# RWKV-style attention and a maxout-like layer on one core: the exponential for k' moved into the PSUM bank of the sums, fp32 sums for three units, a new order

## The chip, the cores and the metric

One core of a Trainium2 chip runs the whole computation as one program. The metric is the device time of the program in microseconds (us), the median of several runs, inputs and outputs in the chip's HBM. TensorE is PE in the profile (its weight loads PEld), VectorE is DVE, ScalarE is ACT, GpSimd is POOL and SyncE is SP; SP issues every DMA of this kernel from one queue, in order.

## The reference

There are 4 batches, 8 heads, 768 tokens and 48 channels a head. A state of 48 x 48 a head runs over the tokens; its output feeds a layer of width 1024.

```python
for t in range(S):                      # S = 768
    cur = einsum('bhd,bhe->bhde', u[None] * kt, vt)
    y[:, :, t] = einsum('bhd,bhde->bhe', rt, state + cur)
    state = wt[..., None] * state + einsum('bhd,bhe->bhde', kt, vt)
x  = y as [B*S, H*D]                    # 3072 x 384
h1 = x @ w1 ; h2 = x @ w2               # 384 x 1024 each
out = maximum(h1, h2) @ w_out           # 1024 x 384
```

All of it is fp32 in HBM; w lies between 0.80 and 0.95.

## The kernel before

The tokens go in three segments of 256, and the work in eight *units* (`UNITS`): units 0 to 3 are segment 0 of one batch each, units 4 and 5 are segment 1 of two batches each, 6 and 7 are segment 2. Two neighbouring tokens share a partition, so that a unit with one batch is one 128-partition tile. Unit 0 alone is worked in two halves of its heads.

For a unit, the steps have short names that the order below uses; the first number behind the name is the unit.

- `load` brings w, k, r, v (384 KB each and batch). `wp` multiplies the two w of a partition, `ln` takes the logarithm in place (tile lg). For units 3 to 7 (`TWO_PARTS`) `hi` and `lo` split that logarithm into two fp16 parts (L200, L202, L413), and the prefix sum `ex` is two fp16 matmuls with a triangular matrix that add up in one PSUM bank (L395, L396); for the others it is one fp32 matmul (L398). 
- `mz` adds the logarithm itself to the sum and puts it in the SBUF tile MZ (L440). `e0` takes the exponential of the sum in place, in the bank (L436); `ie` takes the exponential of minus MZ into the SBUF tile iE (L460). 
- `rw` and `kw` multiply r and k by w for one of the two tokens. `scale` with a 0 makes r' = r times the exponential in the bank (tile rp); `scale` with a 1 makes k' = k times iE (tile kp). 
- `rk`, `ru`, `dg`, `dd`, `di` make the term with u: r k u, summed over channels, put on the diagonal of the mask tile M.
- r' and k' are transposed, on PE with a copy by ACT (`tr`, `te`, tile RK) for units 0 to 4, by DMA on SP's queue (`dt`, L582) for units 5 to 7. `sc` multiplies them (L641), `mk` copies the product under a mask into M on DVE (L650), `ya` multiplies M with v (L688), `yi` adds the state's part (L675), `kv`, `st`, `sm`, `sb` carry the state on. `vb` casts v to bf16.
- `xe` copies the unit's output to xT. The layer follows: max(h1, h2) = h2 + relu(h1 - h2), so `gt` multiplies xT with the difference w1 - w2 (`wdiff`, tile wd_sb; L706), `rl` takes the relu, and `op` adds xT times a folded matrix wc_sb (w2 times w_out; L725) and the relu times w_out (L729) in one bank. `oe` copies it out, `os` stores it.

PSUM has four single banks G (prefix sums, transposes, `gt`, `op`, preparation) and two pairs Y (`sc`, `kv`, the output). In the kernel before, the pools hand the buffers of a tag out.

The list `ORDER` sets the order of the whole program, written out by hand: each word is a step, and each engine takes its own instructions in that order, so what stands ahead on an engine's queue goes first. `@d`, `@a` and `@p` pick DVE, ACT or POOL for a step that may run on more than one; `load`, `dt` and `os` stand on SP's queue.

Of the kernel before, what the change touches and what calls it, by code (L numbers as in the profile page):

```python
# [54 lines left out]
load.0.w.1 load.0.w.0 wp.0.0@d hot.8.2 hot.8.3 load.2.w.0 zero.v.1@d wp.0.1@d mask ln.0.0 tri
zero.k.1@p load.1.w.0 ln.0.1 ex.0.0 load.1.r kw.0.0@d mz.0.0 wp.2.0@d rw.0.0@d load.1.k zero.o@p
load.0.v ie.0.0 uspread utake@a wp.1.0@d ex.0.1 ln.1.0 wload.1.0 mz.0.1 scale.0.1.0.0@p hot.8.0
zero.M.1@p ie.0.1 load.3.w.0 ru.0.0@d dg.0 rw.0.1@p kw.0.1@p scale.0.1.0.1@p wt.0.0 ex.1.0 we.0.0
e0.0.0 e0.0.1 wt.0.1 rk.1.0@d hot.8.5 vb.0.1@p load.2.r zero.v.2@d load.2.k load.1.v mz.1.0 ie.1.0
rw.1.0@d wt.1.0 wload.1.2 ln.2.0 ex.2.0 vb.0.0@a we.0.1 scale.0.0.0.0@d zero.k.0@d kv.0  # L60
scale.0.0.0.1@d tr.0.0.1 dd.0@p mz.2.0 woload.0 we.1.0 ru.1.0@p kw.1.0@p row.2 w2turn.0.0 e0.1.0
scale.1.0.0.0@d st.0.0@a tr.0.0.0 te.0.0.1@a sc.0.0.1.1 sc.0.0.0.1 w2turn.0.1 dg.1 te.0.0.0@a
w2take.0.0@a wload.0.2 load.2.v scale.1.1.0.0@d dd.1@p sb.0.0@a wp.3.0@p tr.1.0.1 e0.2.0 st.0.1
te.1.0.1@a rk.2.0@d zero.M.2@p di.0.0@d ie.2.0 zero.M.0@p rw.2.0@d hot.8.1 wload.1.1 ru.2.0@d
kw.2.0@p scale.2.1.0.0@p sc.0.0.1.0 sc.0.0.0.0 mk.0.0.1.0 vb.1.0@a hot.8.4 mk.0.0.0.0 mk.0.0.1.1
mk.0.0.0.1 vb.1.1@a kv.1 scale.2.0.0.0@d tr.1.0.0 ln.3.0 te.1.0.0@a w2turn.2.1 wdiff.2@p sb.0.1@a
st.1.0@a sb.1.0@a di.1.0@d st.1.1 tr.2.0.0 w2take.0.1@a tr.2.0.1 te.2.0.1@a zero.v.0@d sc.1.0.1.0
w2turn.1.0 wload.0.0 wdiff.0@p w2take.1.0@a sc.1.0.0.0 mk.1.0.1.0 mk.1.0.0.0 sb.1.1@a w2take.2.1@d
w2turn.2.0 w2turn.1.1 w2take.2.0@a hi.3@a ya.0.0.1.0 vb.2.1@a ya.1.0.0.0 sm.0@p sm.1@p wload.0.1
wdiff.1@d ya.1.0.1.0 ya.0.0.0.1 load.3.r trih@a yi.1.0 yi.0.0 ya.0.0.0.0 woload.1 ya.0.0.1.1  # L70
xe.1.0@a xe.0.0@d load.3.k te.2.0.0@a gt.1.3 rl.1.3@a dg.2 rk.3.0@d lo.3@d dd.2@a gt.0.2 rl.0.2@a
wocast.1@p gt.1.1 w2take.1.1@d woload.3 gt.0.0 rw.3.0@p woload.2 rl.0.0@a gt.1.2 load.4.w.0 rl.1.2@a
vb.2.0@p ru.3.0@p gt.0.3 rl.0.3@a ex.3.0 wocast.3@d wocast.2@a wocast.0@a rl.1.1@a di.2.0@d
sc.2.0.1.0 mk.2.0.1.0 gt.0.1 mz.3.0 e0.3.0 kw.3.0@p gt.1.0 dg.3 sc.2.0.0.0 kv.2 st.2.0@a rl.0.1@a
wp.4.0@d ie.3.0 scale.3.0.0.0@d mk.2.0.0.0 wfold.2 sb.2.1@d wfold.0 dd.3@p ln.4.0 load.3.v st.2.1
wfold.1 sb.2.0@d vb.3.0@a wl.2 hi.4@a lo.4@d ya.2.0.0.0 load.4.r rl.1.0@a di.3.0@d vb.3.1@a row.3
ya.2.0.1.0 wctake.1@a we.2 load.4.k wctake.2@a rk.4.0@d wctake.0@a scale.3.1.0.0@p tr.3.0.0 ex.4.0
mz.4.0 tr.3.0.1 ex.4.1 mz.4.1 te.3.0.0@a kv.3 te.3.0.1@a st.3.0@a yi.2.0 xe.2.0@d ie.4.0 op.1.1
oe.1.1@a st.3.1 load.4.v e0.4.0 sb.3.0@a ru.4.0@d gt.2.0 load.5.w.0 rl.2.0@a sc.3.0.0.0 sc.3.0.1.0
vb.4.1@a gt.2.2 op.1.0 rk.4.1@p rw.4.0@d kw.4.0@d scale.4.0.0.0@d scale.4.1.1.0@d scale.4.1.0.0@p  # L80
e0.4.1 rl.2.2@a scale.4.0.1.0@d op.0.1 sb.3.1@a row.4 oe.1.0@a tr.4.1.0 te.4.1.0@a tr.4.1.1 vb.4.0@a
op.0.0 sm.2@p wl.3 mk.3.0.0.0 ya.3.0.0.0 mk.3.0.1.0 ya.3.0.1.0 yi.3.0 oe.0.1@d ru.4.1@p wp.5.0@p
we.3 sm.3@p te.4.1.1@a gt.2.1 xe.3.0@a dg.4 ln.5.0 oe.0.0@d tr.4.0.1 te.4.0.1@a gt.3.0 rl.3.0@a
rl.2.1@a hi.5@a dd.4@d load.5.k kv.4 di.4.0@d sc.4.1.1.0 load.5.r load.5.v rk.5.0@d gt.2.3 rl.2.3@a
gt.3.2 tr.4.0.0 di.4.1@d te.4.0.0@a mk.4.1.1.0 gt.3.3 st.4.0 st.4.1 os.1.0 rl.3.3@a gt.3.1 rl.3.1@a
ru.5.0@p sc.4.1.0.0 rk.5.1@p sc.4.0.0.0 load.6.r sb.4.0@a vb.5.1@a op.2.1 load.6.w.0 lo.5@d wl.4
ex.5.0 mk.4.0.0.0 os.0.0 sb.4.1@a mk.4.1.0.0 oe.2.1@a mz.5.0 e0.5.0 rw.5.0@p ex.5.1 sc.4.0.1.0
load.6.k ru.5.1@p mz.5.1 ya.4.0.0.0 scale.5.0.0.0@d op.2.0 rl.3.2@a op.3.0 mk.4.0.1.0 e0.5.1 os.1.1
scale.5.0.1.0@d dt.5.0.0 ya.4.0.1.0 dt.5.0.1 kw.5.0@d row.5 oe.3.0@d os.3.0 wp.6.0@p ie.5.0
# [708 lines left out]
```

## Time and profile before

| | |
|---|---|
| median of 3 runs | 146.45 us (146.37 to 147.02) |
| the profiled execution | span 147.2 us, 5536 instructions |
| PE busy | 136.8 us (93%) |
| DVE busy | 116.9 us (79%) |
| ACT busy | 90.6 us (62%) |
| POOL busy | 90.0 us (61%) |
| granted TensorE clock, mean | 0.987 |
| DMA | 31.84 MB, mean 216 GB/s |

A busy share is a mean over the span. Matmuls overlap and their ends are modelled: a row's mean duration of one is longer than the step from one to the next. A line number is that of the kernel before; the order and the notes on the change give lines of the changed kernel, which are 9 higher in the functions quoted above.

### The profile page before, as it was taken

What the parts mean: (1) busy time and instruction counts of PE and PEld (TensorE: products, weight loads), DVE (VectorE), ACT (ScalarE), POOL (GpSimd) and SP (SyncE); (2) the same over time, 40 slices, a digit from 0 to 9 for tenths busy, and PEclk for the clock granted to TensorE, in tenths of its full rate; (3) what the DMA queues carried; (4) which work ended last, traced back from release to release, by engine and by line L of the source; (5) the groups of instructions that cost most, each with busy time, mean ns of one, the idle gap of its engine ahead of it and who ended that gap; (6) DMA issues with size and microseconds to landing.
All of it is one profiled execution on the core that took longest, in us unless ns stands there. A gap on an engine that the chain in (4) does not pass through costs nothing.

```text
span 147.2 us, 5536 instructions
## 1 busy us (share of the span) xinstructions
PE 136.8 (93%) x2403; PEld 84.2 (57%) x2404; DVE 116.9 (79%) x162; ACT 90.6 (62%) x164; POOL 90.0 (61%) x106
## 2 busy tenths in 40 slices
PE   5999999779999999999999994999999999999990
PEld 1355755568757666875654562554557545664560
DVE  2489999999999999999999967399967589361511
ACT  4053793997999849999178677367357483227010
POOL 7659979996986299499785909506996900000000
PEclk9999999999999999999999999599999999999999
DMA  4999999999899899997978999799933990051014
GB/s 104 323 325 357 335 401 394 366 286 304 214 241 277 212 226 282 312 255 174 205 192 177 292 251 207 141 138 291 250 136 78 131 271 20 0 210 62 4 56 157
DMA packets 71186, 31.84 MB, mean 216 GB/s; under 512 B 66293, under 2 KB 70390, under 8 KB 71162
## 3 DMA queue, kind: packets, MB, share of 16 engines
q1 hardware_dynamic: 71162, 31.49, 81.2%
q8 instruction: 19, 0.31, 0.8%
q14 instruction: 5, 0.04, 0.2%
...
## 4 chain that ended last, share of the span: by engine, by line
PE 41%; DVE 35%; issue 6%; POOL 6%; DMA 4%; ACT 3%; SPq 2%; DVEq 0%; POOLq 0%; ACTq 0%
PE G L729 12%; DVE M L650 9%; PE G L706 8%; PE G L234 7%; PE G L725 5%; DVE rp L176 4%; DMA lv<-in_v_dram 4%; DVE rku L176 3%; DVE dg L502 3%; POOL kp L180 3%; DVE M L516 3%; PE Y L688 2%; SPq L582 2%; POOL rku L180 2%; PE Y L675 2%
## 5 line engine op out<-in xcount | busy, mean ns | idle before, releaser
L729 PE MATMUL G<-wo_sb,gT 128*128 128x384 bf16 x192 | 35.8, 331 | 0.0
L706 PE MATMUL G<-xT,wd_sb 128*128 128x256 bf16 (+1 forms) x192 | 34.4, 326 | 0.7 <-ACT xT L168 0.6
L650 DVE CAST_PREDICATED M<-mask,Y 128x1024 bf16<-128x1024 int32 (+1 forms) x26 | 28.6, 1131 | 2.8 <-PE Y L641 1.9
L717 ACT ACTIVATE gT<-G 128x512 bf16<-128x512 f32 x43 | 24.5, 601 | 9.8 <-PE G L706 9.6
L729 PEld LDWEIGHTS <-gT 128*128 128x128 bf16 x192 | 19.0, 99 | 12.6 <-issue 0.3
L706 PEld LDWEIGHTS <-wd_sb 128*128 128x128 bf16 x192 | 17.9, 98 | 12.6 <-DVE wd_sb L176 0.6
L180 POOL TENSOR_TENSOR kp<-lk,iE 128x384 bf16<-128x384 f32 x16 | 17.1, 1096 | 9.3 <-DVE lk L176 4.2
L725 PE MATMUL G<-wc_sb,xT 128*128 128x384 bf16 x72 | 15.7, 327 | 0.0
L180 POOL TENSOR_TENSOR rku<-rku,u_b 128x384 f32<-128x384 f32 x14 | 14.5, 1053 | 2.0 <-DVE rku L176 2.0
L234 PE MATMUL G<-S_b 128*128 128x512 bf16 x47 | 13.6, 442 | 1.8 <-DVE S_b L263 1.8
L168 ACT COPY RK<-G 128x1024 bf16<-128x1024 bf16 x12 | 12.1, 1019 | 4.7 <-PE G L565 4.7
L168 ACT COPY osb<-G 128x384 f32<-128x384 f32 x7 | 3.4, 479 | 15.9 <-PE G L729 12.6
L180 POOL TENSOR_TENSOR rku<-lr,lk 128x384 f32<-128x384 f32 x8 | 10.9, 1393 | 2.5 <-DMA lk<-in_k_dram 1.7
L641 PE MATMUL Y<-RK 48*64 48x128 bf16 x384 | 9.0, 220 | 2.6 <-DVE M L650 2.4
L502 DVE TENSOR_REDUCE dg<-rku 128x16 f32<-128x768 f32 x12 | 11.0, 945 | 0.1
L641 PEld LDWEIGHTS <-RK 48*64 48x64 bf16 x384 | 6.2, 106 | 7.8 <-issue 6.7
L168 ACT CAST xT<-Y 128x768 bf16<-128x768 f32 x7 | 7.0, 1025 | 5.3 <-PE Y L675 4.0
L168 ACT CAST S_b<-S_f 64x768 bf16<-64x768 f32 (+1 forms) x14 | 8.7, 624 | 2.3 <-DVE S_f L612 2.0
L176 DVE TENSOR_TENSOR rp<-lr,G 128x768 bf16<-128x768 f32 (+2 forms) x11 | 8.8, 799 | 1.4 <-ACT G L436 1.4
L234 PEld LDWEIGHTS <-S_b 128*128 128x128 bf16 x48 | 5.1, 112 | 8.3 <-issue 3.3
L516 DVE TENSOR_TENSOR M<-identq,gd 128x512 int32<-128x512 int32 x12 | 9.2, 778 | 0.4 <-POOL gd L168 0.3
L168 DVE CAST xT<-Y 128x768 bf16<-128x768 f32 x5 | 5.1, 1017 | 5.5 <-PE Y L688 3.2
...
## 6 DMA issues: line engine op xcount, KB each, us to landing
...
out_dram<-osb SPq DMA_DIRECT2D x14, 192.0 KB, 3.9
...
out_dram<-wb SPq DMA_DIRECT2D x10, 192.0 KB, 2.0
...
```

Source lines behind the costliest of these rows:

```text
L168: (nc.scalar.copy if e == "a" else nc.vector.tensor_copy if e == "d" else nc.gpsimd.tensor_copy)(o, i)
L176: op(o, a, b)
L180: op(o[:, g], a[:, g], b[:, g])
L234: nc.tensor.matmul(t, zz[:, 0:P], zz[:, 0:512], start=True, stop=True)
L502: nc.vector.reduce_sum(s.dg[:, b].rearrange("p i h -> p h i"), s.rku[:, b], axis=AX.X)
L516: (nc.vector if en == "d" else nc.gpsimd).tensor_tensor(out=o, in0=m, in1=g.unsqueeze(3).to_broadcast([P, 2, H, Q // 2]), op=ALU.bitwise_and)
L641: nc.tensor.matmul(t[q * Q:(q + 1) * Q, e, p * P:(p + 1) * P].rearrange("s (i g) -> s i g", i=2), s.kT[d, b, j, y * n + p, q, :], s.rT[d, ...
L650: nc.vector.copy_predicated(t[:, :, 2 * n * y:2 * n * (y + 1)].rearrange("s i (p e) g -> s p e i g", e=2), mask[:, j].bitcast(I32).unsquee ...
L706: nc.tensor.matmul(t[:, m * n * P:(m + 1) * n * P].rearrange("c (b t) -> c b t", t=P), wd_sb[:, ko, fo * P:(fo + 1) * P], s.xT[:, 0:n, ko, :],
L717: nc.scalar.activation(o, i, AF.Relu)
L725: nc.tensor.matmul(t[:, 0:HD], s.xT[:, a, ko, :], wc_sb[:, ko, :], start=(ko == 0), stop=False)
L729: nc.tensor.matmul(t[:, 0:HD], s.gT[:, c:c + P], wo_sb[:, f, :], start=False, stop=(f == FO - 1))
```

## The change

Three tables and the list change, and the code that hands out PSUM. `E_IN_PSUM` now names units 4 to 7: their `ie` writes the exponential of minus MZ for one batch over the sums, into the bank, once r' of that batch has been made (a branch that was in the code, L458 of the changed kernel), and k' of the batch is scaled from the bank. Since POOL reads no PSUM here, all `scale` steps of these units stand on DVE. `TWO_PARTS` names units 6 and 7 alone, so units 3, 4 and 5 take the fp32 matmul and have no `hi` and `lo`. `PLACES` says for each PSUM tile in turn which of the four banks or two pairs it takes. `ORDER` is new as a whole, with the engine of many steps.

```diff
-BANKS = {'G': 4, 'Y': 2}
+PLACES = {
+    'G': ("0123003123120312132120310310303010123012030301203123123021010320310230210130123213201303"
+           "0231203120121301201321320"),
+    'Y': ("01011101011101010110010010101010110100101010"),
+}
...
-E_IN_PSUM = ()
+E_IN_PSUM = (4, 5, 6, 7)
...
-TWO_PARTS = (3, 4, 5, 6, 7)
+TWO_PARTS = (6, 7)
...
 ORDER = """
-ident zero.s.1@p identq@a load.0.k load.0.r zero.m@p identb@p u zero.s.0@d zero.r@d rk.0.0@d
...
+tri zero.o@p mask zero.m@p ident identb@p zero.s.0@d hot.8.5 load.0.w.1 wp.0.1@d zero.M.2@d ln.0.1
...
+    places = {tag: iter(x) for tag, x in PLACES.items()}
+
+    def place(tag):
+        return tag + next(places[tag])
+
     def bank(dt=F32, tag="G"):
-        return ps.tile([P, 512 if dt is F32 else 1024], dt, tag=tag, name=tag, bufs=BANKS[tag])
+        return ps.tile([P, 512 if dt is F32 else 1024], dt, tag=place(tag), name=tag, bufs=1)
 
     def pair(tag="Y"):
-        return ps.tile([P, 2, 512], F32, tag=tag, name=tag, bufs=BANKS[tag])
+        return ps.tile([P, 2, 512], F32, tag=place(tag), name=tag, bufs=1)
```

The order at three places. First DVE at the start of the program, before:

```order
L263 MEMSET S_b 128x768
L249 MEMSET rp_73 128x32x8
L176 TENSOR_TENSOR rku<-lr,lk 128x768
L176 TENSOR_TENSOR lg<-lw 128x192
L254 MEMSET vp_77 128x8x2x8
L255 MEMSET vp_77 128x8x2x8
L176 TENSOR_TENSOR lg<-lw 128x192
L176 TENSOR_TENSOR lw<-lk,lw 128x4x48
L440 TENSOR_TENSOR MZ<-G,lg 128x4x48
```

and of the change:

```order
L272 MEMSET S_b 128x768
L185 TENSOR_TENSOR lg<-lw 128x192
L266 MEMSET M_82 128x512
L449 TENSOR_TENSOR MZ<-G,lg 128x4x48
L185 TENSOR_TENSOR lw<-lr,lw 128x4x48 x2
L185 TENSOR_TENSOR rp_73<-lr,G 128x4x48
L185 TENSOR_TENSOR rp_73<-lw,G 128x4x48
```

The first work on loaded data was r times k of unit 0 and is now the product of the w of half of its heads; that half of w is also the first load on SP, where k and r were, and k is the sixth.

Second SP's queue from the transposes of unit 5 (RK written from rp0 and kp1) to the load of v for unit 6 (lv), with buffer numbers, before:

```order
L582 DMA_TRANSPOSE RK_1678<-rp0_73 128x8x128 x2
L472 DMA row_1714<-MZ_83 1x1024
L743 DMA out_0_dram<-osb_1716 128x384
L743 DMA out_0_dram<-wb_1583 128x384
L582 DMA_TRANSPOSE RK_1678<-kp1_75 128x8x128 x2
L372 DMA lv_2032<-in_v_dram 128x8x96 x2
```

and of the change:

```order
L591 DMA_TRANSPOSE RK_1525<-rp0_73 128x8x128
L381 DMA lk_1604<-in_k_dram 128x8x96 x2
L752 DMA out_0_dram<-osb_1324 128x384
L591 DMA_TRANSPOSE RK_1525<-kp1_75 128x8x128
L381 DMA lr_1771<-in_r_dram 128x8x96 x2
L481 DMA row_1848<-MZ_83 1x1024
L591 DMA_TRANSPOSE RK_1525<-rp0_73 128x8x128
L591 DMA_TRANSPOSE RK_1525<-kp1_75 128x8x128
L752 DMA out_0_dram<-osb_1944 128x384
L381 DMA lv_2078<-in_v_dram 128x8x96 x2
```

The transposes now go batch by batch, and k, r and v of unit 6 (lk, lr, lv) stand among and behind them; before, w, k and r of unit 6 were issued ahead of all of it and v alone behind it.

Third DVE around the scaling of unit 6, before, where r' is the only scaling in these rows:

```order
L176 TENSOR_TENSOR lk_1609<-lk_1609,lw_1570 128x16x48
L516 TENSOR_TENSOR M1_81<-identq_79,gd_1820 128x2x256
L176 TENSOR_TENSOR lr_1553<-lr_1553,lw_1570 128x16x48
L176 TENSOR_TENSOR rp0_73<-lr_1553,G_2025 128x16x48
L650 COPY_PREDICATED M1_81<-mask_71,Y_2068 128x8x2x64
L650 COPY_PREDICATED M1_81<-mask_71,Y_2196 128x8x2x64
L176 TENSOR_TENSOR rp0_73<-lr_1553,G_2038 128x16x48
```

and of the change:

```order
L659 COPY_PREDICATED M1_81<-mask_71,Y_2025 128x8x2x64
L659 COPY_PREDICATED M1_81<-mask_71,Y_2042 128x8x2x64
L185 TENSOR_TENSOR rp0_73<-lr_1771,G_2014 128x16x48
L449 TENSOR_TENSOR MZ_83<-G_2061,lg_1703 128x8x48
L185 TENSOR_TENSOR kp0_74<-lk_1604,G_2014 128x16x48
L177 CAST xT_2205<-Y_2110 128x6x2x64
L185 TENSOR_TENSOR rp0_73<-lr_1771,G_2061 128x16x48
L177 COPY osb_2314<-G_2286 128x384
L728 TENSOR_SCALAR gT_2316<-G_2298 128x512
L185 TENSOR_TENSOR kp0_74<-lk_1604,G_2061 128x16x48
```

k' stands on DVE behind r' of its batch and reads the same bank (G_2014, G_2061); before it stood on POOL and read iE. The products of r and k with w, which stood here on DVE, went to POOL.

More of the change, by code (lines that the diff above doesn't have):

```diff
@@ L53 @@
 ORDER = """
-ident zero.s.1@p identq@a load.0.k load.0.r zero.m@p identb@p u zero.s.0@d zero.r@d rk.0.0@d
[L55 to L89, printed above, removed]
@@ new lines @@
+load.2.k wp.2.0@d hot.8.0 wload.1.1 zero.k.1@p wload.1.2 wload.1.0 ie.1.0 wload.0.2 wload.0.1
+wload.0.0 tr.0.0.1 te.0.0.1@a kw.0.0@d zero.v.2@p scale.0.1.0.0@p wt.1.0 we.1.0 vb.0.1@a vb.0.0@a
+vb.1.0@a load.3.k ru.0.0@d dg.0 hot.8.2 load.3.r vb.1.1@a sc.0.0.1.1 sc.0.0.0.1 identq@d rw.1.0@d
+dd.0@p di.0.0@d woload.0 scale.1.0.0.0@d tr.0.0.0 kv.0 te.0.0.0@a st.0.0@a mk.0.0.1.1 zero.s.1@d
+mk.0.0.0.1 st.0.1 hot.8.1 zero.v.1@p sc.0.0.0.0 rk.1.0@d ru.1.0@d sc.0.0.1.0 woload.1 dg.1 dd.1@d
+kw.1.0@p sb.0.0@a scale.1.1.0.0@p kv.1 tr.1.0.1 ln.2.0 ex.2.0 mz.2.0 row.2 te.1.0.1@a zero.v.0@p
@@ new lines @@
+wdiff.1@d gt.0.1 rl.0.1@a gt.1.1 gt.1.3 rl.1.1@a load.2.v gt.0.0 rl.0.0@a ru.2.0@d dg.2 dd.2@p
+gt.0.2 rl.0.2@a wocast.0@a load.4.w.0 rk.3.0@d load.4.k ru.3.0@d dg.3 load.3.v vb.2.1@p sc.2.0.1.0
+di.2.0@d sm.1@d wocast.2@d wocast.3@d gt.1.0 gt.0.3 sc.2.0.0.0 rl.1.0@a rl.1.3@a wfold.1 wfold.0
+vb.2.0@a dd.3@a mk.2.0.0.0 wctake.1@a sm.0@p mz.3.0 e0.3.0 row.3 ie.3.0 rw.3.0@d wctake.0@a
+scale.3.0.0.0@d load.4.r kv.2 st.2.0@a st.2.1 rl.0.3@d sb.2.0@a sb.2.1@a load.5.w.0 wl.2 wl.3
+kw.3.0@p wfold.2 wctake.2@a scale.3.1.0.0@d mk.2.0.1.0 di.3.0@d load.5.k gt.1.2 rl.1.2@a op.1.1
@@ new lines @@
+vb.3.0@d wp.4.0@p ln.4.0 vb.3.1@p rk.4.0@d tr.3.0.0 load.5.r tr.3.0.1 oe.1.1@a te.3.0.1@a os.1.1
+yi.2.0 ya.2.0.1.0 ya.2.0.0.0 xe.2.0@a ex.4.0 mz.4.0 ex.4.1 gt.2.1 te.3.0.0@a rl.2.1@a trih@a kv.3
+st.3.0@a mz.4.1 e0.4.0 rk.4.1@d rw.4.0@d load.4.v kw.4.0@p scale.4.0.0.0@d load.7.w.0 st.3.1
+sc.3.0.0.0 mk.3.0.0.0 row.4 ru.4.1@p ru.4.0@p sb.3.1@a gt.2.0 rl.2.0@a op.0.1 wp.5.0@p oe.0.1@a
+sb.3.0@a we.2 sm.2@p sc.3.0.1.0 mk.3.0.1.0 op.0.0 e0.4.1 load.5.v scale.4.0.1.0@d op.1.0 ie.4.0
+scale.4.1.0.0@d ya.3.0.0.0 ya.3.0.1.0 yi.3.0 we.3 ie.4.1 scale.4.1.1.0@d tr.4.1.0 oe.1.0@a oe.0.0@a
@@ new lines @@
+sb.4.1@a yi.4.0 ie.5.0 scale.5.1.0.0@d vb.5.0@a ie.5.1 scale.5.1.1.0@d dt.5.1.0 wp.6.0@p yi.4.1
+ya.4.1.1.0 dg.5 dd.5@d di.5.0@d we.4 sm.4@p load.6.r ya.4.0.0.0 rk.6.0@p ya.4.0.1.0 xe.4.0@a
+xe.4.1@a rk.6.1@p rw.6.0@p row.5 op.2.1 kv.5 oe.2.1@a st.5.0 sb.5.0@d ln.6.0 st.5.1 dt.5.0.1
+dt.5.1.1 gt.4.1 rl.4.1@a hi.6@a di.5.1@d oe.3.0@a os.3.0 gt.4.0 lo.6@d gt.4.5 rl.4.5@a sc.5.0.0.0
+kw.6.0@p mk.5.0.0.0 rl.4.0@a sc.5.0.1.0 gt.4.2 sb.5.1@a gt.4.4 rl.4.2@a gt.4.7 rl.4.7@a gt.4.3
+ex.6.0 mk.5.0.1.0 mz.6.0 rl.4.3@a rl.4.4@d gt.4.6 sc.5.1.1.0 sc.5.1.0.0 mk.5.1.1.0 mk.5.1.0.0 ex.6.1
```

59 lines of the change are left out of this document (35 added, 24 removed).

## The prediction

> **What bounds the kernel now.** I read the busy shares in slices first, to see where one engine is full and where it is not.
>
> ```profile
> PE   5999999779999999999999994999999999999990
> PEclk9999999999999999999999999599999999999999
> ```
>
> Each digit is one fortieth of the 147.2 us. PE is the full engine from the tenth slice on, with one hole (the 4, near 90 us) and, right behind it, one slice at half the clock (the 5). So I cut the span there and asked for busy time by stage; the columns are the stage, its length, and then busy time and number of instructions of each engine.
>
> ```profile
> core 0: us, PE busy (x) PEld busy (x) DVE busy (x) ACT busy (x) POOL busy (x), PEclk, DMA share, GB/s
> 0.00:33.00 33.00, 28.79 (x425) 17.03 (x427) 27.61 (x50) 19.89 (x43) 27.95 (x46) 1.00 1.03 322
> 33.00:75.00 42.00, 41.86 (x848) 29.50 (x848) 41.34 (x55) 34.20 (x61) 32.92 (x34) 1.00 1.01 246
> 75.00:85.00 10.00, 9.53 (x138) 4.96 (x136) 9.84 (x14) 7.56 (x14) 7.19 (x7) 1.00 0.85 217
> 85.00:91.00 6.00, 4.06 (x134) 2.57 (x131) 4.28 (x5) 5.01 (x9) 2.78 (x3) 1.00 0.95 227
> 91.00:97.00 6.00, 6.00 (x146) 3.78 (x138) 3.55 (x5) 1.22 (x2) 3.00 (x4) 0.72 0.99 147
> 97.00:144.00 47.00, 46.59 (x727) 26.41 (x724) 29.80 (x37) 22.70 (x39) 16.19 (x16) 1.00 0.50 130
> ```
>
> From 33 us to 144 us PE is busy for 41.86 + 9.53 + 4.06 + 6.00 + 46.59 = 108.0 of 111.0 us. DVE is as full as PE until 85 us and then has room. The six microseconds from 91 ran at a granted clock of 0.72, which cost 6.00 x 0.28 = 1.7 us. So PE's work behind 33 us is 108.0 - 1.7 = 106.3 us at full clock, and 1.9 us of idle time lies between 85 and 91 and about 0.9 elsewhere. The 33 us is the first matmul of the up-projection, and the last matmul ends at 143.85 (two views: PE in order of time, and the last step of the chain):
>
> ```profile
> 33.11 1.14 PE L706 MATMUL G<-xT,wd_sb 128*128 128x256 bf16 x9 [0.60 <-ACT xT L168]
> ```
>
> ```profile
> 143.87 0.56 DVE wb L168
> ```
>
> The end is therefore a sum of four terms: the time of the first up-projection, 106.3 us of PE work, what PE loses, and 147.2 - 143.85 = 3.3 us of tail (last copy and its store). The chain of waits says what the loss between 70 and 92 us is made of:
>
> ```profile
> 72.91 3.91 POOL kp L180 x4
> 76.82 1.08 SPq L582
> ...
> 79.96 6.14 DMA lv<-in_v_dram
> ...
> 86.91 0.47 ACT G L436
> ...
> 88.55 0.95 DVE rp L176
> 89.51 1.15 DVE M L650
> ```
>
> Unit 5's k' is scaled on POOL for 3.9 us; transposes wait for it on SP's queue; the load of v for unit 6 stands behind them and lands after 6.1 us; on ACT the cast of that v stands ahead of an exponential of unit 6; DVE's next product waits for the exponential; and the mask copy of unit 5 stands behind that product. PE, in order of time, shows the price: 1.94 us idle, and then eight matmuls in 2.16 us that cost 1.46 elsewhere.
>
> ```profile
> 90.70 0.42 PE L641 MATMUL Y<-RK 48*64 48x128 bf16 x16 [1.94 <-DVE M L650]
> 91.05 0.66 PE L725 MATMUL G<-wc_sb,xT 128*128 128x384 bf16 x3
> 91.54 2.16 PE L729 MATMUL G<-wo_sb,gT 128*128 128x384 bf16 x8
> ```
>
> The lost clock is 1.7 us, half of 3.4 us. The Trainium skill (TensorE: Matmul & The Clock Gate, "What's actually happening") has the clock at half rate until a busy window of about 3.4 us has passed, which is this loss; but it starts from an idle window of about 3.4 us, and here 1.94 us were enough. By that page a new hole of 2 us would cost 2 us, by this trace 3.6; the sum below has no hole of that length, so both give the same.
>
> **The change, part by part.** First the named edits, by the groups of instructions (shapes apart; busy time, then mean ns of one).
>
> ```profile
> L180 POOL TENSOR_TENSOR kp<-lk,iE 128x384 bf16<-128x384 f32 x16 | 17.1, 1096 | 9.3 <-DVE lk L176 4.2 <-ACT iE L460 3.9 <-issue 1.1
> L176 DVE TENSOR_TENSOR rp<-lr,G 128x768 bf16<-128x768 f32 x8 | 7.6, 944 | 1.4 <-ACT G L436 1.4
> L176 DVE TENSOR_TENSOR kp<-lk,iE 128x768 bf16<-128x768 f32 x2 | 2.2, 1108 | 0.1
> L460 ACT ACTIVATE iE<-MZ 128x768 f32<-128x768 f32 x4 | 3.4, 838 | 1.5 <-DVE MZ L440 1.4
> L436 ACT ACTIVATE G<-G 128x384 f32<-128x384 f32 x11 | 5.3, 485 | 0.3 <-DVE MZ L440 0.2
> L395 PE MATMUL G<-wst 128*128 128x384 f16 x9 | 2.9, 327 | 0.0
> L398 PE MATMUL G<-lg,tri 128*128 128x384 f32 x4 | 1.8, 528 | 0.0
> L413 DVE SCALAR_TENSOR_TENSOR wst<-lg,wst 128x768 f16<-128x768 f32 x4 | 4.9, 1216 | 0.0
> ```
>
> The exponential for k' in the bank: for units 4 to 7 all eight k' products (one per batch) now read PSUM, which POOL does not do in this kernel, so they stand on DVE. POOL loses six of them (12 halves of 1.10 us, 13.2 us). DVE gains eight and loses two. The trace has no such product from PSUM for k'; the nearest row is r' from the bank, 0.944 us, same shape and types, and the SBUF form's 1.108 bounds it above. I take 0.944: 8 x 0.944 - 2 x 1.108 = +5.3 us on DVE. On ACT four exponentials of 0.838 become eight of about 0.485: +0.5 us, in gaps of an engine that is busy for 62% of the span.
>
> fp32 sums for units 3 to 5: DVE loses two remainders of 1.216 and one of half the size, -3.0 us; ACT loses scaled copies. Five pairs of fp16 matmuls become five fp32 ones. The pair takes two rows of 0.327 (which overlap the next), the fp32 one a single row of 0.528, so between 0.13 us cheaper and 0.20 dearer each; I take +0.06 us, 0.3 in all, on PE's path. The Trainium skill (FP8 and Floating Point Precision, "TensorE Precision Notes") gives true fp32 four passes through the array, against two for the pair; by it each swap would cost as much again as the pair, some 0.3 us, and the forecast would be 1.0 us later. The row of 0.528 for 384 columns, against 0.327 for fp16, speaks against four full passes.
>
> Engines reassigned by the order: relu copies (four more on DVE), output copies (seven fewer on DVE), the three weight differences (all on DVE now, two were on POOL) and small ones. Summed by their rows they leave DVE 2 to 3 us heavier in all than before, 119 us against 116.9, and POOL 9 us lighter. A total of 119 bounds nothing; what counts is what stands ahead of which matmul.
>
> Start. The first up-projection needs all three weight differences and both first xT. Ahead of it DVE had the 50 instructions of 27.6 us in the table's first row. Now 46 stand there: two more weight differences (+2.8), one more fill of the state, two of the masked tiles and some small ones came; one copy of xT, one of r k, one of w2, unit 1's k' and the fills of v went, to ACT, to POOL or to a later place. By the rows of their kinds these balance within 0.3 us. What changes is when DVE can begin:
>
> ```profile
> 5.50 0.96 DVE L176 TENSOR_TENSOR rku<-lr,lk 128x768 f32<-128x768 f32 x1 [3.49 <-DMA lr<-in_r_dram]
> ```
>
> ```profile
> lw<-in_w_dram SPq DMA_DIRECT2D x2, 192.0 KB, 3.3
> ```
>
> Before, the first product waited for two full loads until 5.50. Now half of w is issued first (at 0.8) and lands 3.3 us later, at 4.1: 1.4 us earlier. Against it stand products that need k, which is now the sixth load. I take 1.2 us: first up-projection at 31.9. Bounds: 31.0, if the later waits of the start shorten too, and 33.5, if they lengthen by as much as the head gains.
>
> The hole at 90 us. In the new order k' of unit 5 is on DVE right behind r', w of unit 6 is loaded ahead of the transposes and its k between them, and the cast of unit 6's v stands behind both exponentials of r'. POOL's 3.9 us and the wait for v leave the path: -1.9 us idle, -1.7 us clock. What is late next: unit 6's r is issued only behind the first transpose of k' of unit 5, so POOL's products with it (rku, r w, k w) start when it lands, and DVE's r' and k' of unit 6 queue behind them. And unit 7's r stands on SP behind the stores of unit 4. From unit 4's last output projection to k' of unit 7 the steps are: copy 0.56, two issues 1.97, landing 4.7 (the upper of the three values for r in this stage, below), two rku halves 2.67, r w 1.95, two r' 1.9, k' 0.94, with some 0.5 for the store: 15.2 us.
>
> ```profile
> 79.73 2.67 POOL L180 TENSOR_TENSOR rku<-lr,lk 128x384 f32<-128x384 f32 x2
> ```
>
> ```profile
> 95.98 1.97 SPq L372 DMA_DIRECT2D lr<-in_r_dram  x2
> DMA to landing us min/median/max: 4.6/4.6/4.7
> ```
>
> ```profile
> 131.50 5.18 PE G L706 x24
> 136.68 0.49 PE G L725 x3
> 137.17 1.30 PE G L729 x8
> ```
>
> These are POOL in order of time, SP in order of time with the landings of r from 60 to 100 us, and the chain at the end. PE has in the same stretch eight up-projection groups of 0.65 (5.18 for eight), four output groups of 1.79, and some 4.4 us of attention: 16.8 us. The cover is 1.6 us, thin; the banks that hold unit 7's exponentials are the ones that two of unit 6's up-projections want. I put 1.5 us of new PE idle time on units 5 to 7, bounds 0 and 3.6 (one hole like the old one, clock included).
>
> Sum for a profiled execution: 31.9 + 106.3 + 0.3 (fp32) - 0.3 (one prefix sum now ahead of the start) + 0.9 (small idles as before) + 1.5 + 3.3 = 143.9 us. The profiled execution of before took 147.2 and the median of its runs is 146.45; less that 0.75, the forecast is 143.2 us.
>
> **The rivals.** *The hole only moves* (unit 6's or 7's r takes the place of v): 1.9 + 1.7 us come back in place of the 1.5, so 145.3, or 146.8 with both. For it: SP's queue is as strict as before and a load stands behind a transpose again. Against it: the transposes no longer wait for POOL.
>
> *The held bank makes it slower.* Until now a bank with the sums was free after r'; from now on it is held until k', and k' waits for POOL's k w and r w and so for the loads. If the 15.2 us chain is longer than its 16.8 us of cover (landings of 6.1 like v's, not 4.7, are nearly enough), the up-projections that want these banks stop PE at the same place in units 6 and 7: two holes of 3.6 us instead of 1.5, so 143.2 - 1.5 + 7.2 = 148.9. It decides from a chain about 2 us longer on. For it: four banks only, two of them held. Against it: each unit has another pair of banks to go on with.
>
> *All of it goes*: no new idle time, 141.7; for it that DVE has 17 us of room behind 97 us.
>
> **How the numbers follow.** Forecast 0.50; the hole moves 0.20; slower by held banks 0.14; all gone 0.16. Half a per cent, 0.7 us, is about what a measurement of this kernel can tell: faster means under 145.7. Of the forecast nearly all, of the moved hole about four tenths, and all of the clean case lie there: 0.74; within: 0.11; slower: 0.15. The range runs from 140.7 (start at 31.0, little idle) to 146.7 (the moved hole with its bound); the likeliest case alone has 141.5 to 145.3.
>
> **What would show it.** Right: the first matmul of the up-projection near 32 us; no PE idle time over 1 us between 75 and 100 us and a clock of 1.00 there; k' from the bank near 0.94 us on DVE; PE busy time from the first up-projection to the end near 106 us. Wrong: the first up-projection after 33.5 us (the start did not shrink); PE waiting before an up-projection of unit 6 for k' of unit 7 or for r (the held bank); the clock below 1.00 again; or k' above 1.1 us.

## The result and the profile after

The changed kernel takes 152.21 us (median of four runs, 151.49 to 152.73) where the kernel before took 146.41 in the same comparison: 1.039 of it, 95% interval 1.035 to 1.042. It is slower; the forecast was 143.2 us, faster, with a range up to 146.7. Ratios here leave out executions more than 1.5% above the fastest of the same kernel, so a median can stand a little higher than its ratio says.

Two things must be read together. The profiled execution of after has a span of 150.8 us and a time of 152.54: the time is 1.7 us above the span, and so it is, within 0.4, in every kernel that follows. For before the profile shown ahead of the prediction had 147.2, but nine others, timed in one later comparison, had spans of 144.3 to 145.2. So the base from which the prediction counted was an untypical execution, some 2.5 us longer than these.

The page of after, busy tenths of PE and granted clock in 40 slices of 3.8 us:

```profile
PE   5999959879779999999999979799999999999991
PEclk9999999999977999999999999999999999999999
```

The hole near 90 us is shallow now and has full clock. A new one stands at 41 us (the 7 and 7 in the middle of the first row's first half), and behind it the clock falls. By stage (length, then busy time and number of instructions of each engine, clock, DMA share, GB/s):

```profile
0.00:33.00 33.00, 28.28 (x426) 18.15 (x429) 27.78 (x46) 19.58 (x40) 22.85 (x45) 1.00 1.00 309
33.00:42.00 9.00, 6.37 (x78) 4.77 (x78) 8.90 (x9) 6.20 (x12) 6.00 (x7) 1.00 1.02 274
42.00:50.00 8.00, 7.51 (x67) 4.20 (x67) 7.19 (x11) 4.57 (x10) 0.52 (x2) 0.79 0.57 151
50.00:75.00 25.00, 24.97 (x534) 17.59 (x532) 22.35 (x30) 18.61 (x36) 20.02 (x21) 1.00 0.89 215
75.00:85.00 10.00, 9.73 (x278) 5.92 (x275) 9.31 (x14) 8.68 (x16) 6.21 (x6) 1.00 1.06 238
85.00:97.00 12.00, 10.00 (x258) 5.83 (x247) 10.63 (x12) 8.28 (x15) 11.37 (x13) 1.00 1.00 192
97.00:148.00 51.00, 50.56 (x779) 28.82 (x777) 34.38 (x43) 23.36 (x44) 9.02 (x11) 1.00 0.63 151
```

PE lost 2.63 us between 33 and 42 us, nothing of weight from 50 to 85, 2.00 from 85 to 97, and 0.44 in the last 51, nearly all of it behind its last matmul. In 42 to 50 the mean clock was 0.79, which cost 8.00 x 0.21 = 1.7 us. PE in order of time (start, busy time, and in brackets the idle time before and who ended it):

```profile
32.88 0.28 PE L715 MATMUL G<-xT,wd_sb 128*128 128x256 bf16 x1
34.23 3.34 PE L715 MATMUL G<-xT,wd_sb 128*128 128x256 bf16 x29 [1.07 <-DVE wd_sb L185]
...
39.61 0.82 PE L327 MATMUL G<-wo_sb,wb 128*128 128x384 bf16 x4
42.49 3.21 PE L327 MATMUL G<-wo_sb,wb 128*128 128x384 bf16 x12 [2.05 <-DVE wo_sb L177]
45.63 0.63 PE L605 MATMUL Y<-vp,kp 64*64 64x48 bf16 x32
46.19 1.88 PE L327 MATMUL G<-wo_sb,wb 128*128 128x384 bf16 x8
```

The up-projection does one matmul at 32.88 and goes on only at 34.23, when VectorE has made the last weight difference. Then the fold (wfold) does 4 of its 24 matmuls and waits 2.05 us for wo_sb. Behind the wait twelve of them take 3.21 us and eight 1.88; before, all 24 took 4.06. VectorE in the same time shows why wo_sb is late:

```profile
38.25 0.95 DVE L511 TENSOR_REDUCE dg<-rku 128x16 f32<-128x768 f32 x1
39.12 0.97 DVE L525 TENSOR_TENSOR M<-identq,gd 128x512 int32<-128x512 int32 x1
40.02 1.15 DVE L185 TENSOR_TENSOR S_f<-T,W 128x192 f32<-128x192 f32 x1
41.09 1.82 DVE L177 CAST wo_sb<-wso 128x768 bf16<-128x768 f32 x2
```

The two casts (wocast.2, wocast.3) stand in the new order behind unit 3's bonus products and di.2 and sm.1. Before, one was made at 36.31 and the others on ScalarE and GpSimd, and the fold began at 40.02 without a wait. At the old hole, PE again:

```profile
89.72 0.64 PE L650 MATMUL Y<-RK 48*64 48x128 bf16 x32 [0.89 <-DMA RK<-kp]
...
95.06 0.65 PE L738 MATMUL G<-wo_sb,gT 128*128 128x384 bf16 x3
96.82 0.97 PE L738 MATMUL G<-wo_sb,gT 128*128 128x384 bf16 x5 [1.11 <-issue]
```

0.89 us for a turned k', and 1.11 us in the middle of eight matmuls for nothing that the profile shows. The two edits by their groups (busy, mean ns), VectorE and then PE:

```profile
L185 DVE TENSOR_TENSOR kp<-lk,G 128x768 bf16<-128x768 f32 x8 | 7.5, 948 | 0.7 <-ACT G L458 0.6 <-issue 0.2
```

```profile
L407 PE MATMUL G<-lg,tri 128*128 128x384 f32 x14 | 5.9, 516 | 0.0
```

k' from the bank costs 0.948 us, as forecast. An fp32 sum is two of the 14 records.

### The profile page after: what moved, and what is told of

Its sections match the earlier page's. It is cut to its first block, busy times and chain, and to the rows that moved or that the text cites. A ratio compares the mean times of both kernels' runs of the same rounds, so it can differ in the third digit from the quotient of the medians.

```text
span 150.8 us, 5533 instructions
## 1 busy us (share of the span) xinstructions
PE 137.4 (91%) x2401; PEld 85.3 (57%) x2404; DVE 120.5 (80%) x160; ACT 89.4 (59%) x166; POOL 76.0 (50%) x100
## 4 chain that ended last, share of the span: by engine, by line
PE 51%; SPq 21%; DVE 11%; DMA 9%; issue 3%; ACT 2%
PE G L738 17%; SPq L381 13%; PE G L715 11%; PE G L734 7%; DMA lw<-in_w_dram 4%; SPq L299 4%; PE Y L697 3%; PE G L327 3%; DVE dg L511 3%; DMA RK<-kp 3%; SPq L294 3%; DMA lv<-in_v_dram 2%; PE Y L650 2%; DVE rku L185 2%; PE G L407 2%
## 5 line engine op out<-in xcount | busy, mean ns | idle before, releaser
L726 ACT ACTIVATE gT<-G 128x512 bf16<-128x512 f32 x39 | 22.3, 599 | 11.6 <-PE G L715 11.2
L189 POOL TENSOR_TENSOR rku<-lr,lk 128x384 f32<-128x384 f32 x8 | 7.8, 1005 | 12.7 <-DMA lr<-in_r_dram 9.8
L177 ACT COPY RK<-G 128x1024 bf16<-128x1024 bf16 x11 | 11.1, 1020 | 4.3 <-PE G L574 4.3
L189 POOL TENSOR_TENSOR lk<-lk,lw 128x384 f32<-128x384 f32 x6 | 6.7, 1133 | 10.9 <-DVE rku L185 10.9
L177 ACT COPY osb<-G 128x384 f32<-128x384 f32 x12 | 5.6, 477 | 10.8 <-PE G L738 8.6
L177 ACT CAST xT<-Y 128x768 bf16<-128x768 f32 x8 | 8.1, 1025 | 4.3 <-PE Y L684 3.3
L449 DVE TENSOR_TENSOR MZ<-G,lg 128x384 f32<-128x384 f32 (+1 forms) x13 | 6.7, 518 | 4.2 <-PE G L407 3.7
L177 ACT CAST S_b<-S_f 64x192 bf16<-64x192 f32 (+1 forms) x14 | 7.8, 555 | 3.1 <-DVE S_b L272 2.2
L177 ACT COPY wb<-G 128x384 f32<-128x384 f32 x9 | 4.2, 479 | 8.4 <-PE G L738 8.4
L697 PE MATMUL Y<-M,vp 64*32 64x128 bf16 x768 | 8.7, 219 | 0.5 <-issue 0.3
```

What stands on the lines that cost most here:

```text
L177: (nc.scalar.copy if e == "a" else nc.vector.tensor_copy if e == "d" else nc.gpsimd.tensor_copy)(o, i)
L189: op(o[:, g], a[:, g], b[:, g])
L697: nc.tensor.matmul(lhsT=s.vp[g, b, 2 * p + e, j, m * 32:(m + 1) * 32], rhs=s.M[b, j][g, :, 2 * p + e, :], **into(s, b, q, p * 96 + (e + m) ...
L726: nc.scalar.activation(o, i, AF.Relu)
```

## The experiments

Line numbers shift by a few between kernels; the names in the rows stay. A step is written as in ORDER: name, unit, part, and the engine behind the @.

| run | against before (95%) | profiled span |
|---|---|---|
| after | 1.039 (1.035 to 1.042) | 150.8 |
| before again | one time, 146.96 us | 145.2 |
| after, casts on GpSimd | 1.027 (1.021 to 1.032) | 148.4, again 147.7 |
| after, sums ahead of warming | 1.060 (1.056 to 1.065) | 152.7 |
| after, three mends | 1.027 (1.015 to 1.039) | 148.1 |
| after, lighter start | 1.029 (1.022 to 1.036) | 152.0 |
| after, no exponential in the bank | 1.046 (1.038 to 1.054) | 153.0 |
| before, fp32 sums alone | 1.007 (1.004 to 1.010) | 145.7 |
| before, bank exponential alone | 1.083 (1.075 to 1.090) | 156.9 |
| the same, a k' out of turn (two kernels) | 1.079 and 1.091 | 156.1, 156.9 |
| before, bank for unit 4 alone | 1.026 (1.022 to 1.030) | 149.1 |
| the same, further behind | 1.013 (1.010 to 1.017) | 146.6 |
| before, late casts | 1.005 (1.001 to 1.008) | 145.3 |
| before, one cast behind | 0.995 (0.993 to 0.997) | 144.4 |
| before, two steps behind | 0.999 (0.997 to 1.000) | 145.3 |

**What before really has at 90 us.** No edit; a second profile.

> The kernel before, unchanged, profiled a second time. The profiled span of 147.2 us lies 0.8 above its median time, while each later kernel's time is 1.7 to 2.1 us above its own span. Theory A (the first profile of before caught an execution with the 1.94 us wait and the low clock at 85 to 97 us that its usual executions do not have): span 144 to 145 us, granted clock 1.00 there, and the wait at most 1 us. Rival (the wait and the low clock are in every execution): span about 147, clock .86 in 85 to 97 us.

Span 145.2, clock 1.00 until PE's last matmul. PE at the old hole:

```profile
90.09 0.42 PE L641 MATMUL Y<-RK 48*64 48x128 bf16 x16 [1.67 <-DVE M L650]
```

The wait is there (1.67 us, over the 1 us of theory A), but no half clock follows it. Of the 3.6 us that the prediction meant to win, at most 1.7 was there to be won in a usual execution. Of the 52 executions of before that were timed beside the trials, 50 had a mean clock of 0.995 or more and two less (0.988 at a span of 147.3 us, and 0.855).

**The fold's casts.**

```diff
-... wdiff.1@d ... dg.2 dd.2@p ... di.2.0@d sm.1@d wocast.2@d wocast.3@d gt.1.0 ...
+... wdiff.1@d ... dg.2 wocast.3@p wocast.2@p dd.2@p ... di.2.0@d sm.1@d gt.1.0 ...
```

> The changed kernel with one thing taken back: the casts of wo_sb 2 and 3 that the fold reads move from VectorE, where they end at 42.9 us, to GpSimd's idle stretch 33.1 to 36.1 us. Theory A (the fold waits for these two casts, and the wait brings the low clock): the 2.05 us wait at the fold goes, the 20 fold and up-projection matmuls at half clock cost 1.9 us less, so 152.2 - 4 = 148 us, and PE's lag behind its own work at 49 us falls from 21 to 17 us. Rival B (the two named edits, sums in fp32 and the exponential in the bank, are what costs): the wait goes elsewhere, time stays within 1 us of 152.2.

> The changed kernel with the fold's casts on GpSimd, profiled a second time (four executions had spans of 147.7 to 151.8 us at granted clocks of 0.997 to 1.0). Theory A: the spread lies in waits for transfers, at 87 us for the turned k' and in the wait of 1.4 us that shows no releaser near 95 us. Rival: it lies in the start or in half clock. Whichever wait differs from the first profile by over 0.3 us tells.

Median 150.64 us, 1.6 less than after; spans 148.4 and 147.7 in the two profiles, so 2.4 and 3.1 us less, not 4. The stages 33 to 42 and 42 to 50 of the first, to be held against those of after:

```profile
33.00:42.00 9.00, 8.46 (x90) 5.84 (x89) 8.90 (x9) 6.58 (x13) 7.73 (x9) 1.00 0.96 256
42.00:50.00 8.00, 7.42 (x152) 5.12 (x153) 7.04 (x12) 6.39 (x13) 2.26 (x3) 1.00 1.07 262
```

The fold's wait and the low clock are gone: theory A holds for them. Part of it is given back later. PE's waits in the first profile, then in the second:

```profile
33.59 3.34 PE L713 MATMUL G<-xT,wd_sb 128*128 128x256 bf16 x29 [0.43 <-DVE wd_sb L183]
...
87.24 0.64 PE L648 MATMUL Y<-RK 48*64 48x128 bf16 x32 [1.76 <-DMA RK<-kp]
...
94.61 0.97 PE L736 MATMUL G<-wo_sb,gT 128*128 128x384 bf16 x5 [1.38 <-issue]
```

```profile
34.37 3.34 PE L713 MATMUL G<-xT,wd_sb 128*128 128x256 bf16 x29 [1.07 <-DVE wd_sb L183]
...
86.54 0.64 PE L648 MATMUL Y<-RK 48*64 48x128 bf16 x32 [0.55 <-DMA RK<-kp]
...
93.41 0.97 PE L736 MATMUL G<-wo_sb,gT 128*128 128x384 bf16 x5 [0.88 <-issue]
```

The wait for the turned k' differs by 1.2 us between two executions of one kernel, the one without a releaser by 0.5, the start by 0.8 the other way. The spread lies in transfers and in the start, and not in the clock, which is 1.00 in both. Most of the start's share has a visible cause: GpSimd's cast of wo_sb waits for its load, and in the second profile it began at 32.16 us, ahead of VectorE's third weight difference, which then took 1.84 us; in the first it began at 32.95, and the difference, from 32.32 on, took 1.22. (In after the cast began at 32.01, and the third difference took 1.85.)

**The start.** Three trials.

```diff
 sums ahead of warming:  -... zero.s.0@d hot.8.5 load.0.w.1 ... ex.0.1 ...   +... zero.s.0@d load.0.w.1 ... ex.0.1 hot.8.5 ...
 three mends:            -hot.8.5   +hot.5.5;  casts as above;  -dt.5.0.1 dt.5.1.1 (behind st.5.1)   +dt.5.0.1 behind scale.5.0.1.0, dt.5.1.1 behind dt.5.1.0
 lighter start:          -identq@d +identq@a;  -wdiff.2@d +wdiff.2@p ahead of wocast.1@p;  casts as above
```

> The changed kernel with the first sum (ex.0.1) ahead of the eight warming matmuls hot.8.5 on TensorE instead of behind them. Theory A': VectorE's 1.88 us idle at 4.2 to 6.1 us shrinks by about 1.1 us, everything VectorE does up to wdiff.1 comes that much earlier, the first up-projection's 1.07 us wait goes and the time falls by about 1.0 us to 151.2. Rival: the start is set by the transfers of the first 33 us or by the fold's wait anyway, and the time stays within 0.4 us of 152.2.

> The changed kernel with three mends: the casts for the fold on GpSimd, five warming matmuls at the start instead of eight, and the transfers that turn unit 5's second r' and k' issued ahead of load.6.r on SP's queue (they land at 87.2 us now and PE waits 1.8 us). Theory A: the casts give 2.4 us of span as measured, the start 0.5 to 1, the transfers 1 to 1.7: span about 146.0, time 147.5 to 148.5 us. Rival (what is won early is lost again at the next transfer): 149.5 us or more.

> The changed kernel with the fold's casts on GpSimd as before, and VectorE rid of 2.4 us ahead of the first up-projection: identq to ScalarE, wdiff.2 to GpSimd. Theory A (what the start gained at its head was spent on VectorE's added work): first up-projection without a wait at 33.0 us against 34.2 (33.6 with the casts alone), span about 147.8 us. Rival (transfers set the start): first up-projection at 33.6 us or later.

The first, in which the first two places of `PLACES` are swapped too, was 154.95 us: both theories missed. The eight warming matmuls, behind ex.0.1, now hold up the second sum, which starts at 7.97 us (in after both were done by 6.44); the up-projection goes on at 35.92, 1.7 us later than in after. The fold still waits 2.19 us. The second has its first sum at 4.37 us and VectorE's first use of it 0.67 us earlier, but then VectorE waits for r:

```profile
5.39 0.36 DVE L447 TENSOR_TENSOR MZ<-G,lg 128x192 f32<-128x192 f32 x1 [1.02 <-PE G L405]
6.21 0.63 DVE L183 TENSOR_TENSOR lw<-lr,lw 128x192 f32<-128x192 f32 x2 [0.46 <-DMA lr<-in_r_dram]
```

The up-projection goes on at 34.07, 0.16 us earlier than in after. Its transfers, moved ahead, leave a wait of 1.27 us for the turned k' (0.55 and 1.76 in the two profiles without the move) and one of 0.25 without a releaser, yet the time is 152.5 us at the median (149.85 to 153.4), not the 147.5 to 148.5 expected: the rival, on the whole. What the longer executions lost is not seen, as only the shortest was profiled. The third took identq (0.90 us in after) and one weight difference (1.22) off VectorE and gained nothing (152.46 us). Two rows of its VectorE, and then one of its GpSimd:

```profile
16.38 1.33 DVE L523 TENSOR_TENSOR M<-identq,gd 128x512 int32<-128x512 int32 x1 [1.82 <-ACT identq L233]
...
31.07 3.64 DVE L183 TENSOR_TENSOR wd_sb<-gT 128x1024 bf16<-128x1024 f32 x2
```

```profile
30.13 3.50 POOL L187 TENSOR_TENSOR wd_sb<-wst 128x512 bf16<-128x512 f32 x2
```

identq on ScalarE is late, and VectorE waits 1.82 us for it; the two weight differences left on VectorE take 1.42 and 2.29 us beside the third on GpSimd, where in after the three took 1.22, 1.22 and 1.85. That profile also has half clock from 22.1 to 25.5 and from 90.4 to 93.8 us, so its span is not used. The start is bound by several things at once (transfers, VectorE, ScalarE's order); which of them keeps VectorE's last weight difference, and with it the up-projection, at 34 us against the old 33 is not settled.

**The named edits, each alone.**

fp32 sums for units 3 to 5 in the old order:

```diff
-TWO_PARTS = (3, 4, 5, 6, 7)
+TWO_PARTS = (6, 7)
-hi.3@a lo.3@d hi.4@a lo.4@d hi.5@a lo.5@d      (steps of ORDER)
```

> The kernel before, old order, with the fp32 sums for units 3 to 5 alone (hi and lo of units 3, 4, 5 dropped). Theory A (the order as found anew costs, the edit does not): five sums cost 0.05 us more each on PE and VectorE is rid of 2.4 us, ScalarE of 2.2 us: 145 to 146.5 us. Rival B (fp32 sums cost): over 147.5 us.

147.52 us, 0.7% slower: at the rival's bound, and outside theory A's. Unit 3's sum in this kernel, and then its pair in the second profile of before, each with the PE instruction behind it:

```profile
37.15 0.81 PE L395 MATMUL G<-lg,tri 128*128 128x384 f32 x2
37.89 0.42 PE L638 MATMUL Y<-RK 48*64 48x128 bf16 x16
```

```profile
37.14 0.33 PE L395 MATMUL G<-wst 128*128 128x384 f16 x1
37.30 0.33 PE L396 MATMUL G<-wst 128*128 128x384 f16 x1
37.56 0.42 PE L641 MATMUL Y<-RK 48*64 48x128 bf16 x16
```

What a sum costs PE is the step from its start to that of the next instruction, not the length of its records, which overlap the next: 0.74 us here, against 0.42 for the pair. Over the five it is 3.62 against 1.97 us: +1.65 us on PE, 0.33 a sum. VectorE has 2.2 us less to do (113.9 against 116.1), and the wait at 90 us falls from 1.67 to 0.93 us. What is left of the 1.65 is 0.9 us, close to the 1.05 us (0.7%) by which the time rose.

The exponential in the bank in the old order, each ie behind its r', each k' behind that on VectorE:

```diff
-E_IN_PSUM = ()
+E_IN_PSUM = (4, 5, 6, 7)
-... scale.4.0.0.0@d scale.4.1.1.0@d scale.4.1.0.0@p e0.4.1 rl.2.2@a scale.4.0.1.0@d op.0.1 ...
+... scale.4.0.0.0@d ie.4.0 scale.4.1.0.0@d e0.4.1 rl.2.2@a scale.4.0.1.0@d ie.4.1 scale.4.1.1.0@d op.0.1 ...
```

> The kernel before, old order, with the exponential in the bank for units 4 to 7 alone: ie of each half behind r' of that half, k' on VectorE right behind it (three of the k' come from GpSimd). Theory A (the edit is harmless, the new order is not): VectorE takes about 6 us of k' more that GpSimd had at 2 us each, and frees no other work, 145.5 to 148 us. Rival B (the held bank costs): PE stops before sums or up-projections for a G bank, 149 us or more.

> The kernel before, old order, with the exponential in the bank alone, each ie right behind its r' and k' behind that on VectorE, and unit 6's second half ahead of the transfer and of kv that read it (in the run before kv of unit 6 read k' too early). Theory A (ScalarE, in order, stands still at each ie until VectorE has made r', and the ReLU copies behind it hold up PE): 154 to 157 us, with waits of PE on gT and osb from ScalarE of over 4 us in all. Rival (only k' read too early made that time): within 2 us of 146.4.

> The kernel before, old order, with the exponential in the bank alone, each k' behind all that it reads (in the two runs before, k' of unit 5 or 6 was made or read out of turn). Theory A (ScalarE, in order, stands still at each ie until VectorE has made r', and the ReLU copies behind it hold up PE): over 152 us, a wait of PE of some 2.8 us on gT near 55 us. Rival (the two runs were slow because a product was out of turn): within 2 us of 146.4.

In the first, k' of unit 5 was made before its product with w, and the second half of unit 6's k' was read before it was made; in the second only the former. They took 157.9 and 160.0 us, the third, which computes all, 158.63: 12 us slower. The first text's theory A, a harmless edit, is refuted; the last text's holds for the time and for the 2.79 us wait on gT near 55 us. ScalarE's waits in the third (who waited for whom, total, times, longest):

```profile
ACT G L447 <- DVE rp L174: 9.9, 7, 3.1
```

But of PE's 11.2 us of waits behind the start only 5.4 were ended by ScalarE (gT, and a copy of xT); VectorE ended 5.8 (mask copies, k', a copy of xT). So ScalarE's stand is shown for about half, and how much of the other half comes from the k' products that VectorE took over is not separated by these kernels.

For one unit alone, and with both ie behind the next exponential and the next ReLU copy:

```diff
+E_IN_PSUM = (4,)
 unit 4 alone:    as above
 further behind:  +... scale.4.0.0.0@d e0.4.1 rl.2.2@a scale.4.0.1.0@d ie.4.0 scale.4.1.0.0@d ie.4.1 scale.4.1.1.0@d op.0.1 ...
```

> The kernel before with the exponential in the bank for unit 4 alone, each ie right behind its r'. Theory A (ScalarE stands 2.75 us at ie.4.0 until VectorE's r' is done at 54.2 us; the ReLU copy behind it holds PE's output projection 2.79 us): a wait of PE on gT of 2.5 to 2.9 us at 55 us, time 148.5 to 149.5 us, and a quarter or so of the 12 us that units 4 to 7 cost. Rival (the 12 us come from VectorE's added k' in units 5 to 7): within 0.7 us of 146.4.

> The same, unit 4 alone, but both ie behind e0.4.1 and the ReLU copy rl.2.2 on ScalarE, both k' behind both r' on VectorE. Theory A (the price is the place in ScalarE's queue, not the exponential): no wait of PE on gT over 0.5 us near 55 us, time 146.4 to 147.5 us. Rival (the hop ScalarE, VectorE, ScalarE, VectorE itself is the price): within 0.7 us of the run with ie right behind r'.

150.33 and 148.41 us. Unit 4 alone, ScalarE and then PE:

```profile
54.35 0.49 ACT L447 ACTIVATE G<-MZ 128x384 f32<-128x384 f32 x1 [2.76 <-DVE rp L174]
54.78 0.45 ACT L434 ACTIVATE G<-G 128x384 f32<-128x384 f32 x1
55.15 0.59 ACT L715 ACTIVATE gT<-G 128x512 bf16<-128x512 f32 x1
```

```profile
55.79 0.95 PE L723 MATMUL G<-wc_sb,xT 128*128 128x384 bf16 x3 [2.79 <-ACT gT L715]
```

ScalarE stands at the exponential until VectorE has used the bank for r'; the ReLU copy behind it is late, and the output projection that reads the copy waits 2.79 us. With the exponentials further behind, that wait is gone, and PE waits instead for k' itself:

```profile
55.93 0.38 PE L563 MATMUL G<-identb,rp 128*128 128x128 bf16 x4 [1.32 <-DVE kp L174]
```

So both theories hold in part: of 3.8 us, the place in ScalarE's queue made about 1.9 (with half clock, which followed the 2.79 us), and 1.9 stay, which is the longer way ScalarE, VectorE, ScalarE, VectorE (1.8 us of waits for k'). Whether other places in the old order would bring the rest down was not tried.

And in the new order, without the exponential in the bank (ie once for both halves into iE behind both sums):

```diff
-E_IN_PSUM = (4, 5, 6, 7)
+E_IN_PSUM = ()
```

> The changed kernel, new order, with the exponential taken out of the bank: ie once for both halves into iE behind both sums, k' on VectorE where it stood. Theory A (in the new order the bank costs little, the fold's wait most): 151 to 152.5 us, the 2.05 us wait at the fold unchanged. Rival (the exponential in the bank is the cause, by ScalarE's waits for r'): 148 us or less.

153.21 us, a little over theory A's band and not 148: in the order that was found for it, taking the exponential out of the bank wins nothing back. The wait at the fold, 2.06 us, is unchanged.

**The suspected places in the old order.**

```diff
 late casts:       -wocast.3@d wocast.2@a   +... ru.3@p ... dg.3 wocast.2@d wocast.3@d sc.2.0.0.0 ...
 one cast behind:  -load.6.v os.0.1 vb.6.1@a mz.6.0 ... ie.6.0 kw.6.0@d e0.6.0   +load.6.v os.0.1 mz.6.0 ... ie.6.0 kw.6.0@d e0.6.0 vb.6.1@a
 two behind:       as one cast behind, and ie.6.0 between e0.6.0 and vb.6.1@a
```

> The kernel before, old order, with the fold's last two casts put late on VectorE, behind dg.3 (the new order's place), nothing else changed. Theory A (this place alone makes a wait at the fold): PE waits 1.0 to 2.0 us at the first fold matmul for wo_sb from VectorE, the time is 147.5 to 148.5 us, and 1.7 us more in executions where half clock follows. Rival (the old order has slack that takes it up by the wait at 90 us): within 0.7 us of 146.4.

> The kernel before with one step moved: on ScalarE the cast of unit 6's v (vb.6.1), which waits for its load, goes behind the three exponentials of unit 6. Theory A (the chain of waits read in the prediction: cast, exponential, r', mask copy, PE): r' is ready 1.1 us earlier, the 1.67 us wait of PE at 90 us shrinks to about 0.5, time 145.0 to 145.4 us. Rival (the wait is set by POOL's k' and the transposes, the cast is only on top of it): within 0.3 us of 146.4.

> The kernel before with two steps moved on ScalarE: the exponential for k' of unit 6 (ie.6.0) and the cast of its v (vb.6.1) both behind the exponentials that r' needs. Theory A (the chain at 90 us runs through ScalarE's order): r' can start when its product with w is done, 0.2 to 0.6 us earlier than with the cast alone, the wait of 0.66 us falls to 0.1 to 0.4, time 145.7 to 146.0 us. Rival (k' of unit 6 is now late, as GpSimd waits for iE): 146.2 us or more.

Late casts: 147.31 us, 0.5% slower, and PE waited only 0.35 us at the fold, since VectorE came to the casts at 40.54 us there, not 41.09, and made both in 1.03 us, not 1.82. So the trial shows the sign, not the 2 us, and misses both theories: the same two steps at a like place in the list cost little where VectorE is done with them 1.3 us earlier.

One cast behind: 146.17 us against 146.65, 0.995 (0.993 to 0.997). It is the only kernel of this study that is faster than before. The chain read in the prediction is right: with the cast of v out of the way r' started at 87.18 us instead of 87.95 and the wait at 90 us fell by a microsecond:

```profile
89.32 0.42 PE L638 MATMUL Y<-RK 48*64 48x128 bf16 x16 [0.66 <-DVE M L647]
```

The time fell by half of that. The second step brought nothing more: the wait stayed at 0.66 us, and 0.999 is no difference.

## Why the prediction was wrong

Its sum for a profiled execution, term by term, against the profiled execution of after:

| term | forecast | measured |
|---|---|---|
| first up-projection | 31.9 | 34.23 |
| PE work behind it, without the next row | 106.3 - 0.3 | 106.1 |
| fp32 sums | 0.3 | 1.3 |
| half clock | 0 | 1.7 |
| idle time of PE behind the start | 0.9 + 1.5 | 4.3 |
| tail | 3.3 | 3.2 |
| span | 143.9 | 150.8 |
| from the span to the time | -0.75 | +1.7 |

The measured work is what is left between 34.23 and PE's end at 147.6 when 4.3 us of idle time (9.75 in all, 5.43 of it up to 34.23), 1.7 of clock (half of 3.4 us) and 1.3 are taken off. The 1.3 is for the four fp32 sums that stand behind the start: their steps are 1.39 (two together), 0.70 and 0.75 us, 2.84 in all, where four pairs at 0.39 (1.97 for five in the second profile of before) would take 1.6. PE's work, k' at 0.948 us and the shallow hole at 90 us came as forecast. Of the prediction's signs of being wrong two came, the up-projection after 33.5 us and a clock below 1.00, the second at a place that it had not looked at.

**The start** is the first step that failed, by 2.3 us. The head did begin earlier, even more than forecast (VectorE's first product at 3.29 us, not 4.1). But VectorE then stood 1.88 us for the first sum, behind warming matmuls: up to the end of its last weight difference it is idle for 5.22 us, against 5.39 before, so next to nothing of the 1.2 us was kept. And "by the rows of their kinds these balance" was wrong. Up to that end (34.17 us, before 32.67) VectorE is busy for 28.95 us, against 27.28. The first 33 us alone, 27.78 against 27.61, hide this, as the last difference still runs then. Of the 1.7 us more, 0.6 is the third difference, which ran beside GpSimd's cast (1.85 us instead of 1.22). The trials show that removing one wait of the start brings out the next.

**The idle time** was put on the wrong place. The forecast had 1.5 us of new idle time, on units 5 to 7. That part held: behind 50 us PE lost little but the 0.89 and 1.11 us near 90. The 2.05 us at the fold, and the 1.7 us of half clock behind them, were in no term, since the step that moved the two casts behind seven products on VectorE was not costed against the fold that reads them. That was the check to make: each PE step that reads a product of VectorE, with the work ahead of it on both engines, and not only in the stage that had the hole.

**The half clock** was read as the price of any hole of 2 us. It followed the fold's wait, and the mean clock of 0.986 to 0.989 in all four executions of after, against 0.995 to 1.00 in 50 of 52 of before, says that a drop of this size came in each of them. For before it was in the first profile and hardly ever else, so it was not there to be won.

**The base.** Subtracting 0.75 us was wrong by 2.45: the profiled execution was a long one, and the time stands 1.7 us above the span. The half clock that was taken for a regular loss is what made that execution long, so this error and the one above have one root.

**The fp32 sums** were mis-sized: 0.3 us in the sum, 1.3 measured (1.65 for all five in the old order). The prediction set one record of 0.528 us against two of 0.327; but a sum is two records, and the lengths are times in flight, not steps. The Trainium skill (FP8 and Floating Point Precision, "TensorE Precision Notes") has four passes for true fp32. Set against the pair's two matmuls, that is as much again as the pair: 2 x 0.163 us, their step back to back, a sum, or 1.6 us for five, an estimate. The trace agrees (0.33 a sum, 1.65 for five). The prediction had named this rule and set it aside by the length of the record.

**The exponential in the bank** was costed as "+0.5 us, in gaps of an engine that is busy for 62% of the span". Gaps say nothing of a queue in order. Each such exponential waits for r' on VectorE, and with the k' products put there the edit is 12 us in the old order. In the new order little of it is left (after, ScalarE waits there 3.3 us in three waits). It is not what took the room at the fold and at the start: without the bank the fold's wait was 2.06 us and the up-projection went on at 35.47 us, later still.

**The rivals.** The forecast of held banks named another mechanism than what came: no up-projection of unit 6 waited for k' of unit 7. The hole did not move to unit 6's or 7's r, though GpSimd waits 4.4 and 5.4 us for these loads as foreseen, with no loss on PE.

Between the second profile of before and that of after, the fold makes 3.8 us (2.05 of wait, 1.7 of clock), the start 1.2 (33.02 to 34.23), PE's work behind the start 0.5 and the other waits 0.3, together the 5.7 us between the spans. What stays open: why the new order, with the fold mended, still takes 4 us more than before. The two profiles of that kernel are 3.3 and 2.5 us longer than before's second: 0.6 and 1.35 of it in the start, 0.8 and 0.7 in PE's work, where the fp32 sums stand, and 2.0 and 0.6 in waits. What its longer executions (spans of 149.5 and 151.8 us) lost was not caught in a profile.
